# One issue order for the attention's cycle, or one for each of three stages

## The chip, the cores and the metric

The kernel runs on one core of a Trainium2 chip. The metric is the device time of one execution in microseconds (us); the number compared is the median over several runs of the same kernel.

## The reference, cut to what matters

Two branches work on the same 2048 x 640 input and are mixed by a gate per row. Branch A is attention with 32 heads of width 20, branch B is a Fourier mixing: a DFT along the features, then one along the sequence, of which the real part is kept.

```python
g = sigmoid((x * gate_w).sum(-1, keepdims=True))          # x = A_x, 2048 x 640
q, k, v = split(x @ wqkv)                                 # 32 heads of 20
o = softmax(q @ k.T * 20 ** -0.5) @ v                     # per head, 2048 x 2048 scores
a = concat_heads(o) @ wo
f_re, f_im = x @ dft_hid_re.T, x @ dft_hid_im.T           # feature DFT
b = dft_seq_re @ f_re - dft_seq_im @ f_im                 # sequence DFT, real part
return g * a + (1 - g) * b
```

(The input B_x is handed in but not read.)

## The kernel before, in words

The kernel writes its instruction streams by hand: no scheduler reorders anything, and each engine takes its instructions in the order in which the Python code issues them.

After some 270 us of projections (q, k, v and the first tiles of the feature DFT) a loop of 256 cycles follows (L849). It carries the attention and, in the gaps, the Fourier branch and the output projection. An attention "unit" is a pair of heads and half of the queries; there are 32 units of 8 cycles each, a cycle is 4 steps, and a step covers two heads.

One cycle issues four kinds of work to TensorE, in the order of a string of letters, `ORDER` (L36, read in L850 to L856):

- `e` (L830): a score matmul, keys x queries, 128 x 512, whose result ScalarE turns into exp (L832) and writes to the tile `p`. A cycle has 8.
- `m` (L168): a score matmul the other way round, queries x keys, 128 x 512, of which VectorE takes the row maxima (L170). These run `LEAD` = 41 steps ahead of the `e` for the same scores, since the maxima must be known first. A cycle has 8.
- `F` (`fill`, L774): some steps of the other branch. A step is a pair of matmuls of 320 columns, one on each half of the array, that add into the PSUM tiles `yp0` and `yp1`. In the feature DFT (`hid_tile`, L346) a cycle has 15 steps, in the sequence DFT (`dft_step`, L575) 16, and in the output tiles (`out_tile`, L646) 12. The steps of a cycle are spread over the `F` places of the string in equal shares (L759 to L764).
- `B` (`burst`, L836): the 16 matmuls that multiply `p` with `v` (L494), and whatever reads a finished `yp` out (L839; ScalarE reads one half and VectorE adds the other).

Array halves: a head has 20 rows, three copies are stacked to 60 rows (62 with the maxima), and so a score matmul uses 64 of the 128 rows of the array: rows 0 to 63 for one head of the pair ("half 0"), rows 64 to 127 for the other ("half 1"). The two heads of a step are issued one after the other. Which one comes first is set by the table `FIRST` (L37), one entry for each of the four steps of a cycle, read in L816. A fill step has one matmul for each half, half 0 first.

PSUM banks: all scores, `e` and `m` alike, take their banks from one ring of five (`bank`, L122). So score number k of a cycle can be loaded only after ScalarE or VectorE has read score k - 5.

The 256 cycles fall into three stages: 54 cycles beside the feature DFT (`HID` = 54), about 170 beside the sequence DFT (56 products of 3 cycles, and 2 more cycles at the first of them, whose first cycles have fewer steps: `RAMP`, L42), and 30 beside the output tiles. In the last ten cycles no `m` is left to issue.

Of the kernel before, what the change touches and what calls it, by code (L numbers as in the profile page):

```python
# [32 lines left out]

ORDER = "emFemFFFFemFeFFmeFFemFFFmmFFmeeB"  # L36
FIRST = {"e": (0, 0, 1, 1), "m": (1, 1, 1, 1)}  # L37


LEAD = 41  # L40
# [32 lines left out]
def mix_kernel(ctx: ExitStack, tc: tile.TileContext, xa, wqk, wb, cdft, wo, out):  # L73
# [48 lines left out]
    def bank():  # L122
        return ps_w.tile([P, 512], F32, name=f"ps{next(turn) % 5}")
# [23 lines left out]
    def q_unit(n):  # L147
        u = n % 2 * (S // 2)
        return qst[n // 2 % 2][:, u : u + S // 2]
# [8 lines left out]
    def s_mm(i, h):  # L158
        n, s = divmod(i, 32)
        if n >= NU:  # L160
            return lambda: None
        qt, kc = divmod(s, 4)
        q, k = q_unit(n), kst[(n // 2) % 2]
        if n not in mx:
            mx[n] = small.tile([P, 2, 8, 4], F32, name="mx", bufs=2)
        ps = bank()
        b = 64 * h
        pe.matmul(ps, q[b : b + KROWS, qt * P : (qt + 1) * P],  # L168
                  k[b : b + KROWS, kc * 512 : (kc + 1) * 512], start=True, stop=True)
        return lambda: dve.tensor_reduce(mx[n][:, h, qt, kc : kc + 1], ps, axis=AX.X, op=ALU.max)  # L170

    def s_end(i):
        n, s = divmod(i, 32)
        if n < NU and s == 31:
            if now[0] < 0:
                max_nm(n)
            else:
                ends.append(n)
        if s == 1 and 0 < n <= NU and now[0] < 0:
            max_chain(n - 1)  # L180
# [237 lines left out]
    for n, c in enumerate(order):  # L418
        for t in range(4):
            m = 4 * n + t  # L420
# [317 lines left out]
    HID = 4 * NS - HEAD  # L738
# [10 lines left out]
    edge = [first]  # L749
    for u in range(UNITS):  # L750
        k, t = LONG[u // HT], u % HT
        edge.append(edge[-1] + (2 if u == 0 else 0) + 3 + k * (t + 1) // HT - k * t // HT)
    cycles += [(edge[u], edge[u + 1], 3 * NS) for u in range(UNITS)]
    cycles += [(edge[-1] + u, edge[-1] + u + 1, 3 * (ND - 1)) for u in range(2 * len(PRE))]
    assert cycles[-1][1] <= last + 1
    at_goal = 0
    for c0, c1, count in cycles:
        for c in range(c0, c1):
            share = count * (c + 1 - c0) // (c1 - c0) - count * (c - c0) // (c1 - c0)  # L759
            if c0 == first:  # L760
                share = RAMP[c - c0]
            places = ORDER.count("F")
            goals[c] = [at_goal + share * (f + 1) // places for f in range(places)]
            at_goal += share  # L764

    for k, tt in enumerate(PRE):
        i = 4 * (edge[-1] + 2 * k)
# [6 lines left out]
    def fill(c):  # L774
        nonlocal done
        goal = goals[c].pop(0) if c in goals else 0
        while done < goal:
            next(fills)
            done += 1

    def begin(i):
        now[0] = i
        n, s = divmod(i, 32)
        for fn in later.pop(i, ()):
            fn()
        if s % 2 == 0:
            flush()
        if s == 0 and n % 2 == 0:
            p = n // 2
            if p + 1 < NP:  # L790
                at_step(i + 6, functools.partial(load_v, p + 1))
                for j, args in enumerate(load_stack(p + 1)):
                    at_step(i + 2 + j, functools.partial(sp.dma_start, *args))
        if i < total:
            pts[n, s // 2, s % 2] = pair_tile()

    def end(i):
        if start < i <= start + HT:
            for k in range(2):
                at_step(i + 3, load_a(0, 2 * (i - start - 1) + k))  # L800
        if i % 4 == 2:
            c = i // 4
            if c + HEAD in (NS, 2 * NS):
                at_step(i + 2, load_wb(3 + (c + HEAD) // NS, pool, pool))
            if c in (HID - 7, HID - 5, HID - 3):
                at_step(i + 4, load_c((c - HID + 7) // 2))
        if i in LAST:
            LAST[i]()
# [3 lines left out]
    def score(kind):  # L812
        x = heads[kind]
        heads[kind] += 1
        i, z = divmod(x, 2)
        h = z ^ FIRST[kind][(i - (LEAD if kind == "m" else 0) - 1) % 4]  # L816
        if kind == "m":
            s_mm(i, h)()
            if z:
                s_end(i)  # L820
            return
        if z == 0 and i <= total:
            begin(i)
        if i < total:
            n, s = divmod(i, 32)
            kt, qc = divmod(s, 2)
            q, k = q_unit(n), kst[(n // 2) % 2]
            b = 64 * h
            pt = bank()
            pe.matmul(pt, k[b : b + KROWS + 2, kt * P : (kt + 1) * P],  # L830
                      q[b : b + KROWS + 2, qc * 512 : (qc + 1) * 512], start=True, stop=True)
            act.activation(pts[n, kt, qc][:, h], pt, AF.Exp, scale=float(DH) ** -0.5)  # L832
            if z:
                end(i)

    def burst(c):  # L836
        for n in ends:
            max_nm(n)
        run_extras(max(done - HIDS, 0) // 3, 2)  # L839
        for kt in (2 * c, 2 * c + 1):  # L840
            av_step(now[0], kt // NS, kt % NS)
        while ends:
            max_chain(ends.pop(0))
        if c == HID - 1:
            start_dft()

    for kind in "emme":
        score(kind)
    for c in range(total // 4):  # L849
        for kind in ORDER:  # L850
            if kind == "F":
                fill(c)
            elif kind == "B":
                burst(c)
            else:
                score(kind)  # L856
# [124 lines left out]
```

## Time and profile before

| | |
|---|---|
| median of 3 runs | 1891.77 us |
| lowest, highest run | 1891.42, 1894.12 us |
| span of the profiled execution | 1888.5 us |
| TensorE matmul busy | 1877.4 us (99% of the span) |
| VectorE, ScalarE, GpSimd busy | 1470.0, 1219.1, 1005.1 us |
| DMA | 280.50 MB, mean 149 GB/s |

The times are device times of whole executions; the span runs from the first to the last instruction in one profiled execution, and that execution has no other time of its own in the page. What lies around the span is put at 1891.77 - 1888.5 = 3.3 us here.

In the profile's rows, PE is a matmul and PEld the load of its weights. The engine letters are PE (TensorE), DVE (VectorE), ACT (ScalarE), POOL (GpSimd), SP (the queue that issues most DMAs). A row of the timeline gives the start in us, the time from the first start to the last end of the merged instructions, engine, line, operation, tiles and how many. A matmul's time in a row is longer than its turn on the array, because consecutive matmuls overlap; the turn is read from the distance between starts.

### The profile page before, as it was taken

What the parts mean: (1) busy time and instruction counts of PE and PEld (TensorE: products, weight loads), DVE (VectorE), ACT (ScalarE), POOL (GpSimd) and SP (SyncE); (2) the same over time, 40 slices, a digit from 0 to 9 for tenths busy, and PEclk for the clock granted to TensorE, in tenths of its full rate; (3) what the DMA queues carried; (4) which work ended last, traced back from release to release, by engine and by line L of the source; (5) the groups of instructions that cost most, each with busy time, mean ns of one, the idle gap of its engine ahead of it and who ended that gap; (6) DMA issues with size and microseconds to landing.
All of it is one profiled execution on the core that took longest, in us unless ns stands there. A gap on an engine that the chain in (4) does not pass through costs nothing. (4 is left out here: it accounts for less than half of the span.)

```text
span 1888.5 us, 44537 instructions
## 1 busy us (share of the span) xinstructions
PE 1877.4 (99%) x17453; PEld 1358.2 (72%) x17453; DVE 1470.0 (78%) x2445; ACT 1219.1 (65%) x2350; POOL 1005.1 (53%) x872
## 2 busy tenths in 40 slices
PE   9999999999999999999999999999999999999998
PEld 8987777777776677776767677776767677766666
DVE  4145569989898888888888888888888888889954
ACT  4221147777777767666767667666767676677785
POOL 1200001010004999466699989958879988734343
PEclk9999999999999999999999999999999999999999
DMA  7843341221215575536557576736475746442214
GB/s 232 181 133 128 128 154 48 62 76 49 75 58 147 163 238 178 148 123 169 180 176 238 171 234 190 201 119 189 156 220 195 225 147 205 154 114 70 62 49 157
DMA packets 174804, 280.50 MB, mean 149 GB/s; under 512 B 44303, under 2 KB 106895, under 8 KB 174595
## 3 DMA queue, kind: packets, MB, share of 16 engines
q1 hardware_dynamic: 173635, 275.70, 47.7%
q0 software_dynamic: 960, 1.97, 0.6%
q8 instruction: 137, 2.24, 0.5%
q14 instruction: 72, 0.59, 0.1%
HBM read 213.37 MB, written 63.52 MB: 147 GB/s over the span
## 5 line engine op out<-in xcount | busy, mean ns | idle before, releaser
L170 DVE TENSOR_REDUCE mx<-ps 128x1 f32<-128x512 f32 x2048 | 1294.8, 684 | 175.8 <-PE ps L168 154.8
L832 ACT ACTIVATE p<-ps 128x512 f32<-128x512 f32 x2048 | 1087.0, 599 | 432.7 <-PE ps L168 223.6
L168 PE MATMUL ps<-kst,qst 60*128 60x512 f32 x2048 | 785.2, 415 | 3.7 <-DVE mx L170 1.7
L830 PE MATMUL ps<-qst,kst 62*128 62x512 f32 x2048 | 698.9, 413 | 0.5 <-ACT p L832 0.3
L575 PE MATMUL yp<-a,part 64*128 64x320 f32 x5376 | 649.1, 307 | 0.0
L575 PEld LDWEIGHTS yp<-a,part 64*128 64x128 f32 x5376 | 582.2, 186 | 7.3
L494 PE MATMUL av<-p,v 128*21 128x512 f32 x4096 | 491.3, 596 | 0.0
L830 PEld LDWEIGHTS ps<-qst,kst 62*128 62x128 f32 x2048 | 335.7, 185 | 200.9 <-DVE mx L170 182.4
L168 PEld LDWEIGHTS ps<-kst,qst 60*128 60x128 f32 x2048 | 371.2, 184 | 24.7 <-DVE mx L170 9.6
L113 POOL TENSOR_TENSOR part<-raw,part 128x1024 fp32r<-128x1024 f32 (+1 forms) x129 | 290.4, 2251 | 10.3
L494 PEld LDWEIGHTS av<-p,v 128*21 128x21 f32 x4096 | 98.4, 100 | 226.7 <-issue 223.2
L346 PE MATMUL yp<-wb,xs 64*128 64x320 f32 x1920 | 236.0, 308 | 0.1
L112 POOL CAST part<-raw 128x1024 fp32r<-128x1024 f32 (+1 forms) x129 | 127.0, 985 | 161.5 <-PE yp L575 141.2
L346 PEld LDWEIGHTS yp<-wb,xs 64*128 64x128 f32 x1920 | 206.0, 186 | 4.5 <-DVE raw L355 0.5
L465 POOL TENSOR_TENSOR raw<-raw,raw 128x1024 f32<-128x1024 f32 x77 | 185.4, 2408 | 6.4 <-DMA raw<-in_cdft 4.8
L112 POOL CAST wb<-raw 128x966 fp32r<-128x966 f32 (+1 forms) x4 | 3.4, 862 | 255.4 <-DMA raw<-in_wb 255.4
L524 POOL TENSOR_TENSOR o<-o,rb 128x512 f32<-128x512 f32 x31 | 40.2, 1296 | 146.6 <-DMA rb<-r_scr 100.8
L113 POOL TENSOR_TENSOR a<-araw,a 128x320 fp32r<-128x320 f32 x112 | 97.6, 872 | 9.0
L113 DVE TENSOR_TENSOR p<-ps,p 128x512 fp32r<-128x512 f32 x40 | 27.5, 691 | 93.5 <-ACT p L110 90.8
L646 PE MATMUL yp<-a,part 64*128 64x320 f32 x720 | 89.5, 309 | 0.0
L110 ACT ACTIVATE p<-ps 128x512 fp32r<-128x512 f32 x40 | 23.7, 597 | 100.6 <-PE ps L118 100.6
L646 PEld LDWEIGHTS yp<-a,part 64*128 64x128 f32 x720 | 76.9, 186 | 2.5
(86 smaller groups left out, 1237.0 us busy)
## 6 DMA issues: line engine op xcount, KB each, us to landing
raw<-in_cdft SPq DMA_DIRECT2D x192, 512.0 KB
araw<-a_scr SPq DMA_DIRECT2D x192, 160.0 KB
qk_scr<-p SPq DMA_DIRECT2D x40, 512.0 KB
kst<-qk_scr SPq DMA_DIRECT2D x90, 160.0 KB
qst<-qk_scr SPq DMA_DIRECT2D x90, 160.0 KB
a_scr<-raw SPq DMA_DIRECT2D x64, 160.0 KB
yt<-y_scr SPq DMA_DIRECT2D x64, 160.0 KB
y_scr<-yt SPq DMA_DIRECT2D x64, 160.0 KB
```

What stands on the lines that cost most here:

```text
L112: e1.tensor_copy(dst1, src)
L113: e2.tensor_tensor(dst2, src, f32(dst1), op=ALU.subtract)
L168: pe.matmul(ps, q[b : b + KROWS, qt * P : (qt + 1) * P], k[b : b + KROWS, kc * 512 : (kc + 1) * 512], start=True, stop=True)
L170: return lambda: dve.tensor_reduce(mx[n][:, h, qt, kc : kc + 1], ps, axis=AX.X, op=ALU.max)
L346: pe.matmul(yp[h][:, :HE], xs[r, xz, d, cs], w[r, wz, d, :HE], start=d == 0 and z == 0, stop=d == ND - 1 and z == 2)
L465: pool.tensor_tensor(raws[0], raws[0], raws[1], op=ALU.add if PRODUCTS[n][0][1][0] > 0 else ALU.subtract)
L494: pe.matmul(av[32 * j : 32 * j + DH + 1, :], v[:, kt, h * (DH + 1) : (h + 1) * (DH + 1)], pp[qc][:, h, :], start=kt == 0, stop=kt == NS - 1)
L524: pool.tensor_tensor(o, o, rb, op=ALU.mult)
L575: pe.matmul(yp[h][:, :HE], c[r, cz, cs], a[r, az], start=s == 0 and z == 0, stop=s == NS - 1 and z == 2)
L646: pe.matmul(yp[h][:, :HE], o[r, oz, d], wos[d, hf][r, wz], start=d == 0 and z == 0, stop=d == ND - 2 and z == 2)
L830: pe.matmul(pt, k[b : b + KROWS + 2, kt * P : (kt + 1) * P], q[b : b + KROWS + 2, qc * 512 : (qc + 1) * 512], start=True, stop=True)
L832: act.activation(pts[n, kt, qc][:, h], pt, AF.Exp, scale=float(DH) ** -0.5)
```

## The change

Instead of one order and one table for all 256 cycles there are three, chosen by the cycle's number: for the feature DFT (`hid`), the sequence DFT (`seq`) and the output tiles (`out`). Each has its own string and its own choice of which array half each step takes first. The number of `F` places differs (9, 7 and 13 instead of 15), so a place takes more than one step. The counts of every kind of instruction stay as they were.

```diff
-ORDER = "emFemFFFFemFeFFmeFFemFFFmmFFmeeB"
-FIRST = {"e": (0, 0, 1, 1), "m": (1, 1, 1, 1)}
+ORDERS = {
+    "hid": ("emFmeFFemFeFmeFemFFmeFmmeB", {"e": (0, 0, 1, 1), "m": (1, 1, 1, 0)}),
+    "seq": ("ememFFemFemFmeFemFFmeemB", {"e": (1, 1, 1, 1), "m": (0, 0, 0, 0)}),
+    "out": ("ememFFFFemeFFmeFFemFFFmmFFmeeB", {"e": (0, 0, 1, 1), "m": (1, 1, 1, 1)}),
+}
...
+    def play(c):
+        return ORDERS["hid" if c < HID else "seq" if c < edge[-1] else "out"]
+
...
-            places = ORDER.count("F")
+            places = play(c)[0].count("F")
...
-        h = z ^ FIRST[kind][(i - (LEAD if kind == "m" else 0) - 1) % 4]
+        c, k = divmod(i - (LEAD if kind == "m" else 0) - 1, 4)
+        h = z ^ play(c)[1][kind][k]
...
-        for kind in ORDER:
+        for kind in play(c)[0]:
```

Written out with the half behind each score, and with as many F as there are steps (one F is a pair of matmuls, one for each half), a full cycle of each stage is issued like this:

```
hid before  e0 m1 F e1 m0 FFFF e0 m1 F e1 FF m0 e1 FF e0 m1 FFF m0 m1 FF m0 e1 e0 B
hid after   e0 m1 F m0 e1 FFFF e0 m1 F e1 FF m0 e1 FF e0 m1 FFF m0 e1 FF m0 m1 e0 B
seq before  e0 m1 F e1 m0 FFFF e0 m1 F e1 FF m0 e1 FF e0 m1 FFF m0 m1 FFF m0 e1 e0 B
seq after   e1 m0 e0 m1 FFFF e1 m0 FF e0 m1 FFF m0 e1 FF e0 m1 FFFFF m0 e1 e0 m1 B
out before  e0 m1 e1 m0 FFFF e0 m1 e1 FF m0 e1 FF e0 m1 FF m0 m1 FF m0 e1 e0 B
out after   e0 m1 e1 m0 FFF e0 m1 e1 FF m0 e1 FF e0 m1 FFF m0 m1 FF m0 e1 e0 B
```

(With 12 steps on 15 or 13 places some places of the string stay empty in the output stage.)

## The prediction

> **What bounds the kernel now.** I read the page first, its busy shares and its two costliest groups.
>
> ```profile
> span 1888.5 us, 44537 instructions
> PE 1877.4 (99%) x17453; PEld 1358.2 (72%) x17453; DVE 1470.0 (78%) x2445; ACT 1219.1 (65%) x2350; POOL 1005.1 (53%) x872
> L170 DVE TENSOR_REDUCE mx<-ps 128x1 f32<-128x512 f32 x2048 | 1294.8, 684 | 175.8 <-PE ps L168 154.8
> L832 ACT ACTIVATE p<-ps 128x512 f32<-128x512 f32 x2048 | 1087.0, 599 | 432.7 <-PE ps L168 223.6
> L575 PE MATMUL yp<-a,part 64*128 64x320 f32 x5376 | 649.1, 307 | 0.0
> ```
>
> PE is covered by matmuls, and both readers of the scores wait for PE. But "busy" counts a matmul from its start to its last result, and a matmul on one half of the array hides idle time on the other. So 99% proves neither that the array is full nor that nothing else holds it up. For that I need single cycles.
>
> Next the busy time by stretch: the cycles beside the feature DFT, beside the sequence DFT, and the first of the output stage. Under it the same stretches for line L494 alone, whose matmuls come 16 to a cycle.
>
> ```profile
> 269.00:603.30 334.30, 334.19 (x3298) 237.56 (x3294) 299.93 (x505) 245.99 (x485) 34.41 (x22) 1.00 0.26 76
> 628.00:1686.30 1058.30, 1058.30 (x10691) 751.72 (x10689) 888.64 (x1476) 740.44 (x1412) 847.57 (x681) 1.00 0.58 178
> 1692.40:1790.00 97.60, 97.60 (x896) 65.36 (x896) 89.31 (x152) 74.71 (x146) 39.49 (x50) 1.00 0.28 80
> ```
>
> ```profile
> 269.00:603.30 334.30, 101.48 (x848) 20.21 (x848) 1.00 0.26 76
> 628.00:1686.30 1058.30, 319.76 (x2672) 63.63 (x2672) 1.00 0.58 178
> 1692.40:1790.00 97.60, 30.63 (x256) 6.09 (x256) 1.00 0.28 80
> ```
>
> The columns are the stretch, its length, then busy time and count of PE, PEld, DVE, ACT, POOL (in the second answer PE and PEld only), the granted clock, DMA share and GB/s. Cycles: 848 / 16 = 53 of 6.31 us, 2672 / 16 = 167 of 6.34 us, 256 / 16 = 16 of 6.10 us. In the long stretch DVE is busy 84%, POOL 80%, ACT 70%; the clock is full. What one cycle loses or gains there counts about 165 times, so that stage decides.
>
> Now one cycle of the sequence DFT, PE's rows of the timeline; the second fence holds three rows of the same cycle from the timeline of all engines.
>
> ```profile
> 902.16 0.49 PE L830 MATMUL ps<-qst,kst 62*128 62x512 f32 x1
> 902.16 0.49 PE L168 MATMUL ps<-kst,qst 60*128 60x512 f32 x1
> 902.50 0.31 PE L575 MATMUL yp<-a,part 64*128 64x320 f32 x2
> 902.64 0.39 PE L168 MATMUL ps<-kst,qst 60*128 60x512 f32 x1
> 902.64 0.39 PE L830 MATMUL ps<-qst,kst 62*128 62x512 f32 x1
> 902.88 0.75 PE L575 MATMUL yp<-a,part 64*128 64x320 f32 x8
> 903.47 0.39 PE L830 MATMUL ps<-qst,kst 62*128 62x512 f32 x1
> 903.47 0.43 PE L168 MATMUL ps<-kst,qst 60*128 60x512 f32 x1
> 903.70 0.46 PE L575 MATMUL yp<-a,part 64*128 64x320 f32 x3
> 903.88 0.39 PE L830 MATMUL ps<-qst,kst 62*128 62x512 f32 x1
> ...
> 906.29 0.42 PE L830 MATMUL ps<-qst,kst 62*128 62x512 f32 x2
> 906.64 1.92 PE L494 MATMUL av<-p,v 128*21 128x512 f32 x16
> ```
>
> ```profile
> 902.73 4.53 DVE L170 TENSOR_REDUCE mx<-ps 128x1 f32<-128x512 f32 x7 [1.16 <-PE ps L168]
> 902.75 3.24 ACT L832 ACTIVATE p<-ps 128x512 f32<-128x512 f32 x6 [1.24 <-PE ps L168]
> 903.40 0.18 PEld L168 LDWEIGHTS ps<-kst,qst 60*128 60x128 f32 x1
> ```
>
> The prices are in it. A fill takes (0.75 - 0.307) / 3 = 0.148 us of its half (8 fills are 4 on each half). A score takes 903.70 - 903.47 = 0.23. The first pair after the burst takes 902.50 - 902.16 = 0.34, since its weights load in the open: 0.11 more. So each half needs 8 x 0.23 + 16 x 0.148 = 4.21 us plus 0.11. It had 906.29 - 902.16 + 0.23 = 4.36, or 4.39 for the later of the last two (their row is 0.42 long, a single one 0.39). **Only 0.04 to 0.07 us of a cycle is lost between the burst's end and the next burst**; the rest is work, or lies at the edges of the burst, where both strings have scores on either side.
>
> The one place where the scores nearly wait: score 5 (counting from 0; the `m` at 903.47) needs the bank of score 0. Its exp starts at 902.75 and lasts 0.599, so until 903.35; the weights load at 903.40; the matmul starts at 903.47, together with its neighbour. The bank came just in time.
>
> **The change, part by part.**
>
> *Sequence DFT, 165 full cycles.* The new order opens with four scores and four fill steps, and then wants score 5: one fill step earlier than before. The output stage already opens so (`e0 m1 e1 m0 FFFF e0 m1`), and its rows, from the timeline of all engines, show the cost:
>
> ```profile
> 1737.42 0.50 PE L830 MATMUL ps<-qst,kst 62*128 62x512 f32 x1
> 1737.42 0.73 PE L168 MATMUL ps<-kst,qst 60*128 60x512 f32 x2
> 1737.99 0.75 PE L646 MATMUL yp<-a,part 64*128 64x320 f32 x8
> 1738.01 3.12 ACT L832 ACTIVATE p<-ps 128x512 f32<-128x512 f32 x6 [0.90 <-PE ps L168]
> 1738.58 0.39 PE L830 MATMUL ps<-qst,kst 62*128 62x512 f32 x1
> 1738.67 0.18 PEld L168 LDWEIGHTS ps<-kst,qst 60*128 60x128 f32 x1
> 1738.67 0.50 PE L168 MATMUL ps<-kst,qst 60*128 60x512 f32 x1
> 1739.01 0.39 PE L830 MATMUL ps<-qst,kst 62*128 62x512 f32 x1
> 1739.15 0.18 PEld L168 LDWEIGHTS ps<-kst,qst 60*128 60x128 f32 x1
> ```
>
> Time from the first score: score 4 starts at 1738.58 - 1737.42 = 1.16, as 0.34 + 0.23 + 4 x 0.148 gives. Score 5 could start then too, but the first exp ends at 1738.01 + 0.60 = 1738.61 and its weights load at 1.25. Matmul and load start together, it is 0.50 long instead of 0.39, and the next score of that half comes 1739.01 - 1738.67 = 0.34 later instead of 0.23. The half loses 0.09 + 0.11 = 0.20. In the new sequence order score 5 is `m0`: half 0 loses 0.20. Behind the blocked load stand all later matmuls of PE's program, but half 1 has score 4 to work on until 1.39.
>
> Score 7 (`m1`) needs the bank of score 2, the second exp. Half 1 reaches it at 1.16 + 0.23 + 2 x 0.148 = 1.69. In the rows above score 7 also waits for the second exp and loads at 1739.15 - 1737.42 = 1.73, in the open: 0.04 + 0.11 = 0.15 lost on half 1. (Before, score 7 came at 904.14 or later, 1.98 from the start, by its row further down in the same answer:)
>
> ```profile
> 904.14 0.39 PE L168 MATMUL ps<-kst,qst 60*128 60x512 f32 x1
> ```
>
> After that nothing is late by these prices but perhaps the last `m1`. It needs the sixth exp, that of score 10. Half 0 starts score 10 at 1.36 + 3 x 0.23 + 7 x 0.148 = 3.09; an exp starts some 0.48 after its score (902.75 - 902.16 less the 0.11), so it ends near 4.17, and the load may go at 4.22; half 1 wants to start that matmul at 4.24. That is as tight as 903.40 to 903.47 above, and I count nothing for it here.
>
> Sum: half 0 needs 4.21 + 0.11 + 0.20 = 4.52, half 1 4.47. The burst waits for the later one: 4.52 against 4.36 to 4.39 is 0.13 to 0.16 us per cycle; I take 0.14, and 165 x 0.14 = 23.1 us.
>
> What the new order does better is that every fill step finds both halves level. Before, half 1 had a score ahead in most of the cycle. That can be worth at most the loss of 0.04 to 0.07 found above, and 4.52 already contains it as won.
>
> The readout of `yp` comes on every third cycle only and, since four scores now precede the first fill, has 0.23 more time than before: nothing. The tail ends in `m1` instead of `e1 e0`: DVE's last maximum starts later, but its bank is used again only by the fifth score after the burst (at 1.16), more than 2 us away, as the burst alone lasts 1.92: nothing. ACT's last exp comes earlier: nothing, it isn't on the path. The `e` steps that carry the DMA issues on SP stay in the same cycle and move by some tenths of a us; SP's queue and POOL (80% busy, with its loads issued cycles ahead) aren't near a bound, and a slower cycle gives both more room.
>
> *Feature DFT, 54 cycles.* Written out with its steps, the order differs in two swaps: scores 2 and 3, and scores 12 and 14 (`m1 .. e1` become `e1 .. m1`). Each is a swap of equal matmuls. Score 7 now needs the second maximum's bank instead of the second exp's. If that wait just bites, it costs up to the 0.11 of an open load, 54 x 0.11 = 6 us; on the other side, a cycle of 15 steps should take 6.34 - 0.148 = 6.19 and takes 6.31, so at most 0.12 x 54 = 6.5 us could be won, if the earlier last exp lets the readout end sooner. The row nearest to it is score 5's just-in-time load, at a cost near nothing: I take 0.
>
> *Output tiles, 30 cycles.* One step moves from before score 4 to after score 9. Score 5 still waits for the first exp to 1.25, so the moved step's time turns into waiting, and later scores have 0.148 more air. Between -0.148 and +0.148 on 20 cycles, 3 us either way: I take 0. The last ten cycles have no `m`: nothing.
>
> Total: 1888.5 + 23.1 = 1911.6 for the profiled execution, and with the 3.3 us between its span and the median, **1914.9 us**.
>
> **The rivals.**
>
> *The halves decide (faster).* If the banks come free in time, 0.04 is won in 165 cycles: 1891.8 - 6.6 = 1885.2. It decides if the first two exps free their banks 0.2 us earlier than in the rows above. For it: the new order is visibly the more even. Against it: the first exp cannot start before the first score has ended, in any order, and both stages show the same 1.24 to 1.25. The Trainium skill ("TensorE: Matmul & The Clock Gate", Part 3) says that matmuls start and end strictly in program order. By that rule an uneven order would idle a half, and evening it out would be the gain. The trace disagrees: the program has one step, two fills, between the `m` at 903.47 and the `e` at 903.88, but three fills start in between, so one half ran past the other. And the rule could not give more than the measured loss, 1885 again. Chance 0.12 for both.
>
> *Waits without the open load.* If the delayed scores load behind other work, score 5 costs 0.09 and score 7 0.04: half 0 needs 4.41, that is 0.02 to 0.05 or so more, with some unevenness 0.06: 165 x 0.06 = 10, 1902. Against it: the 0.50 and the 0.34 above. Chance 0.17.
>
> *A third wait.* If the last `m1` loads in the open or other scores miss their bank too, up to 0.11 more: 165 x 0.25 = 41, 1933. Chance 0.11.
>
> *No effect:* gains elsewhere cancel it, or the order isn't what I read: 1892. The written-out programs do differ as shown. Chance 0.04.
>
> **How the numbers follow.** Forecast 1914.9 with 0.56. Range 1898 to 1927: it takes in 0.04 to 0.21 us per cycle, so most of the second rival and half of the third. Runs of this kernel agree within 0.14%, so I call under 0.2% (3.8 us) the same. Faster 0.12, same 0.04, slower 0.84.
>
> **What would show it.** In the sequence stage the first `m` behind the four steps starts with its load, about 1.25 after the cycle's first score and 0.50 long; another at about 1.73; from first score to burst 0.13 to 0.16 more than 906.64 - 902.16 = 4.48; 6.47 to 6.50 us per cycle; the other stages at 6.31 and 6.10. I am wrong if cycles of the sequence stage are no longer than 6.34, or if score 5 loads before 1.1.

## The result, and the profile after

The changed kernel takes 1918.06 us (median of 4 runs, 1914.93 to 1921.49), the kernel before 1892.94 us in the same comparison. The ratio is 1.0132, 95% interval 1.0118 to 1.0147: 25.1 us slower, where 23.1 were forecast.

The page of the changed kernel, the lines that answer to those shown of before:

```profile
span 1912.8 us, 44634 instructions
PE 1901.4 (99%) x17453; PEld 1366.3 (71%) x17453; DVE 1450.9 (76%) x2445; ACT 1248.5 (65%) x2350; POOL 1005.3 (53%) x872
L175 DVE TENSOR_REDUCE mx<-ps 128x1 f32<-128x512 f32 x2048 | 1280.8, 683 | 228.9 <-PE ps L173 216.1
L842 ACT ACTIVATE p<-ps 128x512 f32<-128x512 f32 x2048 | 1116.8, 599 | 422.7 <-PE ps L173 347.0
```

The shares hardly move. PE is "99% busy" in a kernel that spends 24 us more; the shares alone don't show where. (The lines have moved: L840 is the score `e`, before L830; L173 is `m`, before L168; L580 the sequence fills, before L575; L842 the exp; L499 the product with v.)

The busy time by stretch, all engines, and below it line L499 alone; the stretches are those of before, moved by what came ahead of them.

```profile
269.00:602.30 333.30, 333.30 (x3297) 234.44 (x3295) 294.80 (x506) 248.37 (x485) 34.41 (x23) 1.00 0.26 76
627.50:1710.60 1083.10, 1083.10 (x10690) 763.05 (x10689) 875.29 (x1476) 767.65 (x1412) 846.44 (x679) 1.00 0.57 174
1716.60:1814.00 97.40, 97.40 (x893) 65.25 (x893) 89.15 (x152) 74.12 (x146) 39.38 (x50) 1.00 0.28 80
```

```profile
269.00:602.30 333.30, 101.47 (x848) 20.18 (x848) 1.00 0.26 76
627.50:1710.60 1083.10, 319.75 (x2672) 63.59 (x2672) 1.00 0.57 174
1716.60:1814.00 97.40, 30.63 (x256) 6.09 (x256) 1.00 0.28 80
```

The same 53, 167 and 16 cycles as before. Feature DFT 333.3 us instead of 334.3, output stage 97.4 instead of 97.6, sequence DFT 1083.1 instead of 1058.3. That stage is 24.8 us longer, and the whole span 24.3; a cycle takes 6.49 us instead of 6.34.

One cycle of that stage, PE's timeline, and then the loads and exps of the same cycle from the timeline of all engines:

```profile
895.12 0.49 PE L840 MATMUL ps<-qst,kst 62*128 62x512 f32 x1
895.13 0.72 PE L173 MATMUL ps<-kst,qst 60*128 60x512 f32 x2
895.47 0.40 PE L840 MATMUL ps<-qst,kst 62*128 62x512 f32 x1
895.69 0.76 PE L580 MATMUL yp<-a,part 64*128 64x320 f32 x8
896.28 0.39 PE L840 MATMUL ps<-qst,kst 62*128 62x512 f32 x1
896.36 0.50 PE L173 MATMUL ps<-kst,qst 60*128 60x512 f32 x1
896.51 0.65 PE L580 MATMUL yp<-a,part 64*128 64x320 f32 x4
896.85 0.49 PE L173 MATMUL ps<-kst,qst 60*128 60x512 f32 x1
897.00 0.39 PE L840 MATMUL ps<-qst,kst 62*128 62x512 f32 x1
...
899.17 0.61 PE L173 MATMUL ps<-kst,qst 60*128 60x512 f32 x2
899.40 0.40 PE L840 MATMUL ps<-qst,kst 62*128 62x512 f32 x1
899.73 0.63 PE L499 MATMUL av<-p,v 128*21 128x512 f32 x4
```

```profile
895.71 1.65 ACT L842 ACTIVATE p<-ps 128x512 f32<-128x512 f32 x3 [1.05 <-PE ps L173]
896.36 0.18 PEld L173 LDWEIGHTS ps<-kst,qst 60*128 60x128 f32 x1
896.85 0.18 PEld L173 LDWEIGHTS ps<-kst,qst 60*128 60x128 f32 x1
```

Score 4 starts 896.28 - 895.12 = 1.16 us after the first score. Score 5 loads at 1.24, just behind the end of the first exp (895.71 + 0.60 = 896.31), in the open, and its matmul lasts 0.50 instead of 0.39. Score 7 does the same at 1.73. From the first score to the burst: 899.73 - 895.12 = 4.61, before 4.48.

In all 167 cycles the mean from the first score to the burst is 4.615 us (before 4.466), from the burst's start to the next first score 1.871 in both. Scores of 0.47 us or longer, a mark of a load in the open, are 2.1 a cycle before (the pair after the burst) and 4.0 after.

### The profile page after: what moved, and what is told of

Its sections match the earlier page's. It is cut to its first block, busy times and chain, and to the rows that moved or that the text cites. A ratio compares the mean times of both kernels' runs of the same rounds, so it can differ in the third digit from the quotient of the medians.

```text
span 1912.8 us, 44634 instructions
## 1 busy us (share of the span) xinstructions
PE 1901.4 (99%) x17453; PEld 1366.3 (71%) x17453; DVE 1450.9 (76%) x2445; ACT 1248.5 (65%) x2350; POOL 1005.3 (53%) x872
## 5 line engine op out<-in xcount | busy, mean ns | idle before, releaser
L175 DVE TENSOR_REDUCE mx<-ps 128x1 f32<-128x512 f32 x2048 | 1280.8, 683 | 228.9 <-PE ps L173 216.1
L842 ACT ACTIVATE p<-ps 128x512 f32<-128x512 f32 x2048 | 1116.8, 599 | 422.7 <-PE ps L173 347.0
L173 PE MATMUL ps<-kst,qst 60*128 60x512 f32 x2048 | 798.1, 432 | 3.9 <-DVE mx L175 1.7
L840 PE MATMUL ps<-qst,kst 62*128 62x512 f32 x2048 | 752.3, 410 | 0.8 <-ACT p L842 0.3
L580 PE MATMUL yp<-a,part 64*128 64x320 f32 x5376 | 585.5, 306 | 0.0
L580 PEld LDWEIGHTS yp<-a,part 64*128 64x128 f32 x5376 | 525.8, 186 | 21.0
L840 PEld LDWEIGHTS ps<-qst,kst 62*128 62x128 f32 x2048 | 352.2, 185 | 198.3 <-DVE mx L175 145.6
L499 PE MATMUL av<-p,v 128*21 128x512 f32 x4096 | 491.3, 596 | 0.0
L173 PEld LDWEIGHTS ps<-kst,qst 60*128 60x128 f32 x2048 | 357.5, 184 | 32.1 <-DVE mx L175 9.1
L499 PEld LDWEIGHTS av<-p,v 128*21 128x21 f32 x4096 | 98.3, 100 | 224.2 <-issue 220.7
L351 PEld LDWEIGHTS yp<-wb,xs 64*128 64x128 f32 x1920 | 202.1, 186 | 4.5 <-DVE raw L360 0.2
L651 PE MATMUL yp<-a,part 64*128 64x320 f32 x720 | 89.9, 310 | 0.0
L651 PEld LDWEIGHTS yp<-a,part 64*128 64x128 f32 x720 | 77.8, 186 | 2.6
```

The costliest lines, as they stand in the source:

```text
L173: pe.matmul(ps, q[b : b + KROWS, qt * P : (qt + 1) * P], k[b : b + KROWS, kc * 512 : (kc + 1) * 512], start=True, stop=True)
L351: pe.matmul(yp[h][:, :HE], xs[r, xz, d, cs], w[r, wz, d, :HE], start=d == 0 and z == 0, stop=d == ND - 1 and z == 2)
L499: pe.matmul(av[32 * j : 32 * j + DH + 1, :], v[:, kt, h * (DH + 1) : (h + 1) * (DH + 1)], pp[qc][:, h, :], start=kt == 0, stop=kt == NS - 1)
L580: pe.matmul(yp[h][:, :HE], c[r, cz, cs], a[r, az], start=s == 0 and z == 0, stop=s == NS - 1 and z == 2)
L651: pe.matmul(yp[h][:, :HE], o[r, oz, d], wos[d, hf][r, wz], start=d == 0 and z == 0, stop=d == ND - 2 and z == 2)
L840: pe.matmul(pt, k[b : b + KROWS + 2, kt * P : (kt + 1) * P], q[b : b + KROWS + 2, qc * 512 : (qc + 1) * 512], start=True, stop=True)
```

## The experiments

The theory under test: a score that wants its bank before the bank's reader is done loses that wait plus an open load, and nothing else in the new order costs. The rivals: the choice of array halves, the other two stages, the grouping of the fills, the string's ends. "Halves" and "string" below are the table and the letters of the sequence stage. A cycle's mean from first score to burst, over 167 sequence cycles of each trace, is called its head; the scores of 0.47 us or longer in a cycle are its open loads.

| run | ratio to before, 95% interval | head, us | open loads |
|---|---|---|---|
| before | 1 | 4.466 | 2.1 |
| after | 1.0132 [1.0118, 1.0147] | 4.615 | 4.0 |
| x2_halves_only | 0.9996 [0.9986, 1.0005] | 4.466 | 2.1 |
| x3_string_only | 1.0287 [1.0270, 1.0305] | 4.789 | 5.0 |
| x4_opening | 1.0122 [1.0107, 1.0137] | 4.594 | 3.1 |
| x5_opening_short6 | 1.0017 [1.0007, 1.0026] | 4.476 | 2.1 |
| x6_short12 | 1.0005 [0.9995, 1.0015] | 4.463 | 2.1 |
| x7_short1236 | 0.9979 [0.9970, 0.9988] | 4.440 | 2.1 |
| x9_step_moved | 1.0129 [1.0114, 1.0144] | 4.609 | 3.0 |
| x11_seq_spaced | 0.9982 [0.9973, 0.9991] | 4.442 | 2.1 |

**Which stage (x1_seq_old).** The changed kernel with the old order in the sequence stage:

```diff
-    "seq": ("ememFFemFemFmeFemFFmeemB", {"e": (1, 1, 1, 1), "m": (0, 0, 0, 0)}),
+    "seq": ("emFemFFFFemFeFFmeFFemFFFmmFFmeeB", {"e": (0, 0, 1, 1), "m": (1, 1, 1, 1)}),
```

> The new orders in the feature DFT and output stages, the old order and halves in the sequence stage. Theory (two bank waits in the sequence stage carry all of it): the 25 us are gone; the traces of before and after put the feature stage at -1.1 us and the output stage at 0, so 0.999 of before, about 1892. Rival (part of the loss is carried over from the other stages or sits at the stage borders): 1897 or more.

1892.39 us, ratio 1.0000 [0.9990, 1.0009]. All of the loss is in the sequence stage; the other two new orders cannot be told from the old ones.

**Halves or string (x2_halves_only, x3_string_only).** Before, with half of the new sequence order each:

```diff
-    "seq": (old string, {"e": (0, 0, 1, 1), "m": (1, 1, 1, 1)}),
+    "seq": (old string, {"e": (1, 1, 1, 1), "m": (0, 0, 0, 0)}),                        # x2
+    "seq": ("ememFFemFemFmeFemFFmeemB", {"e": (0, 0, 1, 1), "m": (1, 1, 1, 1)}),      # x3
```

> Before, but in the sequence stage the new table of array halves (e always half 1 first, m always half 0 first) with the old string. Theory (the waits come from when a bank is wanted, so from the string): sequence cycles stay near 6.31, total within 4 us of before, 1889 to 1897. Rival (the choice of halves makes the loss): most of the 25 us, 1905 or more. Rival (even halves are a gain that the string spoils): up to 0.04 us in 165 cycles, 1886.

> Before, but in the sequence stage the new string with the old table of halves. Theory: score 5 still waits for the first exp at 1.25 us from the first score and score 7 for the second at 1.73, so at least the 25 us: 1917, and if the uneven halves (two scores of one half behind each other after the third group of fills) cost as well, up to 1930. Rival (the halves make the loss): near 1893.

x2: 1891.38 us, no difference. x3: 1946.45 us, twice the loss, and outside of what I expected. So the string makes the loss, and the new halves do no harm but save about half of what this string would cost with the old ones. (With the old string the new table is nearly a mirror image: written out, x2 is the cycle of before with half 0 and half 1 exchanged, but for the last four `e`.) The trace of x3 says why it is slower still (PE, one cycle, first score at 904.49; below it a row of ACT):

```profile
907.28 0.41 PE L840 MATMUL ps<-qst,kst 62*128 62x512 f32 x2
...
908.78 0.40 PE L840 MATMUL ps<-qst,kst 62*128 62x512 f32 x1
908.85 0.50 PE L173 MATMUL ps<-kst,qst 60*128 60x512 f32 x1
909.27 0.63 PE L499 MATMUL av<-p,v 128*21 128x512 f32 x4
```

```profile
907.71 1.09 ACT L842 ACTIVATE p<-ps 128x512 f32<-128x512 f32 x2 [0.31 <-PE ps L840]
```

Two `e` start together at 2.79, one on each half, so that their exps, the fifth and the sixth, queue. The sixth ends at 907.71 + 1.09 = 908.80, 4.31 from the start, and the last score, which needs its bank, loads in the open at 4.36, the fifth open load of the cycle. With the new halves the sixth exp ends at 4.11 (median of the cycles of after).

**Taking the first two waits away by the order (x4_opening).** Before, with the new halves and the new string behind the old opening:

```diff
+    "seq": ("emFemFFFFemFFemFFFmeFFemFFFFmeemB", {"e": (1, 1, 1, 1), "m": (0, 0, 0, 0)}),
```

> Before, but in the sequence stage the new halves and the new string with the old opening: em F em FFFF em, then FF em FFF me FF em FFFF me em. Scores 4 and 5 are wanted at 1.31 us, scores 6 and 7 at 1.84, when their banks (1.25, 1.73) are free. Theory (the two waits are the whole loss): cycles back at 6.31 or a little below, total 1886 to 1894. Rival (pairs of e and m level on both halves make one score after another wait for its reader; the next would be score 9, which needs the third exp): half or more of the loss stays, 1905 to 1917, and the trace shows the first two waits gone and open loads (matmuls of 0.5 us) at later scores.

1914.73 us, ratio 1.0122: the rival, in its time. But the wait that counts is not at score 9. From the timelines of PE and of all engines, rows of one cycle:

```profile
899.70 0.50 PE L840 MATMUL ps<-qst,kst 62*128 62x512 f32 x1
...
901.02 0.40 PE L840 MATMUL ps<-qst,kst 62*128 62x512 f32 x1
901.02 0.42 PE L173 MATMUL ps<-kst,qst 60*128 60x512 f32 x1
901.26 0.48 PE L580 MATMUL yp<-a,part 64*128 64x320 f32 x4
901.55 0.39 PE L173 MATMUL ps<-kst,qst 60*128 60x512 f32 x1
...
902.22 0.44 PE L840 MATMUL ps<-qst,kst 62*128 62x512 f32 x1
...
903.61 0.63 PE L840 MATMUL ps<-qst,kst 62*128 62x512 f32 x2
903.87 0.50 PE L173 MATMUL ps<-kst,qst 60*128 60x512 f32 x1
```

```profile
903.22 0.60 ACT L842 ACTIVATE p<-ps 128x512 f32<-128x512 f32 x1
903.87 0.18 PEld L173 LDWEIGHTS ps<-kst,qst 60*128 60x128 f32 x1
904.29 0.14 PEld L499 LDWEIGHTS av<-p,v 128*21 128x21 f32 x8 [0.24 <-issue]
```

Scores 4, 5 and 7 start on time. Score 9 (902.22) lasts 0.44 instead of 0.39 and so loses little. The last score would go behind the score ahead of it on its half, at 903.61 + 0.23 = 903.84; it needs the bank that the sixth exp reads until 903.22 + 0.60 = 903.82, loads in the open at 903.87 and holds the burst up until 904.29. In all, x4's head is 0.128 us longer than that of before, nearly as much as with the two open loads of the changed kernel (0.148).

**Freeing single banks (x5_opening_short6, x6_short12, x7_short1236).** Some exps of each sequence cycle take half of their columns, so that their bank is free about 0.2 us earlier: in x5 the sixth, in the kernel of x4_opening; in x6 the first two and in x7 the first, second, third and sixth, both in the changed kernel. The product with `v` reads the 256 columns that are there twice, so the matmuls that PE issues stay as many and as long; the result leaves out the other half of these scores. The lines of the exp (those of the product with `v` are not shown):

```diff
-            act.activation(pts[n, kt, qc][:, h], pt, AF.Exp, scale=float(DH) ** -0.5)
+            cut = HID <= (i - 1) // 4 < edge[-1] and 2 * ((i - 1) % 4) + z in (5,)     # (0, 1); (0, 1, 2, 5)
+            w = 256 if cut else 512
+            act.activation(pts[n, kt, qc][:, h, :w], pt[:, :w], AF.Exp, scale=float(DH) ** -0.5)
```

> The kernel of x4_opening, but the sixth exp of every cycle in the sequence stage takes 256 of its 512 columns (the p times v matmul then reads these 256 twice); its bank comes free some 0.25 us earlier. In x4_opening the first two waits were gone and only the last score of a cycle still loaded in the open, 4.17 us from the first, when score 10's bank (read by the sixth exp) came free. Theory (that third wait alone is what is left of the loss): cycles at 6.31, total 1888 to 1896. Rival (the level pairs cost in their middle): 1905 to 1915.

> The changed kernel, but the first two exps of every cycle in the sequence stage take 256 of 512 columns, so that scores 5 and 7 find their banks free. Theory (three waits stand behind each other, each worth about the same): the last score now waits for the sixth exp as in x4_opening, and 1908 to 1917 stays. Rival (the prediction's: these two waits are all): 1886 to 1895.

> The changed kernel, but the first, second, third and sixth exps of every cycle in the sequence stage take 256 of 512 columns. Theory (the loss is nothing but scores that wait for the reader of their bank): all waits are gone and the string is as good as the old one, 1884 to 1895. Rival (something else in the new string costs, such as the order at the edges of the burst): 1900 or more.

x5: 1895.73 us, ratio 1.0017. The third wait was most of what was left in x4; about 3 us over before stay. x6: 1892.86 us, ratio 1.0005. Here my revised theory failed and the recorded prediction held: freeing the first two banks brings everything back, and the third wait doesn't bind. The rows of x6 (first score at 891.45; L845 is the score `e` here, L851 the exp) show why:

```profile
892.05 0.66 ACT L851 ACTIVATE p<-ps 128x256 f32<-128x256 f32 x2 [1.09 <-PE ps L173]
892.62 0.40 PE L845 MATMUL ps<-qst,kst 62*128 62x512 f32 x1
892.63 0.39 PE L173 MATMUL ps<-kst,qst 60*128 60x512 f32 x1
...
893.12 2.27 ACT L851 ACTIVATE p<-ps 128x512 f32<-128x512 f32 x4 [0.41 <-PE ps L845]
...
895.43 0.18 PEld L173 LDWEIGHTS ps<-kst,qst 60*128 60x128 f32 x1
...
895.61 0.39 PE L173 MATMUL ps<-kst,qst 60*128 60x512 f32 x1
```

The short exps release score 5 with score 4, at 1.18. Scores 4 to 11 run 0.14 to 0.18 earlier than in x4_opening (medians of the cycles), and the last four at about the same time, since one more fill step stands ahead of them. The third to the sixth exp run back to back (one row, of four), so that the sixth is done at 893.12 + 2.27 = 895.39, 3.94 from the start instead of 4.12 in x4_opening, and the last score's load at 895.43 is hidden. x7: 1888.00 us, ratio 0.9979 [0.9970, 0.9988]: with these four exps short the new string takes 0.027 us a cycle less than the old one. What x5 and x6 keep over x7, 0.036 and 0.024 us a cycle, fits score 9, which waits for the third exp: it lasts 0.43 us in both (median), and 0.39 in x7, where that exp is short.

**The opening by itself (x9_step_moved).** Before, with one fill step moved from ahead of score 2 to behind score 5, old halves:

```diff
-    "seq": ("emFemFFFFemFeFFmeFFemFFFmmFFmeeB", ...
+    "seq": ("ememFFFFemFFeFFmeFFemFFFmmFFFmeeB", ...
```

> Before, but in the sequence stage one fill step is moved from between the first two pairs of scores to behind score 5: em em FFFF em FF e FF m e FF em FFF mm FFF m e e, old halves. Theory (a score 5 that is wanted before 1.25 us costs its half 0.20, and the later half sets the cycle): +0.13 to 0.16 us per cycle, 1912 to 1918. Rival (one wait on one half is made up by the free running of the halves): up to 1900.

1916.42 us, ratio 1.0129 [1.0114, 1.0144]. One fill step, moved from ahead of score 2 to behind score 5, makes as large a loss as the whole change: score 5 loads 1.24 from the start (one cycle, timeline of all engines):

```profile
897.91 0.50 PE L840 MATMUL ps<-qst,kst 62*128 62x512 f32 x1
...
899.15 0.18 PEld L173 LDWEIGHTS ps<-kst,qst 60*128 60x128 f32 x1
899.16 0.50 PE L173 MATMUL ps<-kst,qst 60*128 60x512 f32 x1
```

**Orders without waits (x10_hid_out, x11_seq_spaced, x12_all_spaced, x13_hid_seq).** Orders laid out so that, by the prices, fewer scores are wanted before their bank is free. x10 has new ones in the feature and the output stage, x11 in the sequence stage, x12 in all three, x13 in the feature and the sequence stage:

```diff
+    "hid": ("ememFFFeFFmeFFFmeFFmeFFFmmFFmeeB", {"e": (1, 1, 0, 0), "m": (0, 0, 1, 1)}),
+    "seq": ("ememFFFFeFFmFemFFeFFmeFFmFmFFeemB", {"e": (0, 0, 0, 0), "m": (1, 1, 1, 1)}),
+    "out": ("emFemFFFeFmeFFmeFmFemFmFmFeeB", {"e": (1, 1, 1, 0), "m": (0, 0, 1, 1)}),
```

> Before, with other orders in the feature DFT (em em FFF e FF me FFF me FF me FFF mm FF m e e) and in the output stage, laid out so that by the prices of the rows (0.23 a score, 0.148 a fill, 0.11 an open load, 1.25 and 1.73 us for the first two exps' banks) fewer scores wait; the sequence stage as before. Theory (a score's wait for its bank is the one loss that an order can take away): the feature cycles shrink from 6.25 towards 6.18 and the output cycles by up to 0.02, 54 x 0.07 + 20 x 0.02 = 4 us, 1886 to 1891. Rival (the feature cycles' 0.06 lie elsewhere): 1892.

> Before, with a sequence order that opens like the changed kernel (four scores, four fill steps) but puts a single e next and score 5 two steps later (em em FFFF e FF m F em FF e FF me FF m F m FF e e m). Theory (the opening costs nothing by itself; what costs is the wait): no open loads after the burst's first pair, 0.02 to 0.04 us won in 165 cycles, 1885 to 1890. Rival (an opening of four scores costs by itself): 1900 or more.

> The orders of x10_hid_out and x11_seq_spaced together. Theory: the two gains add up, 1881 to 1887, a version faster than both kernels. Rival: no gain, 1892.

> The feature order of x10_hid_out and the sequence order of x11_seq_spaced, the output stage with its old order. In x12_all_spaced the feature cycles took 6.21 us (before 6.29 in the runs of that chip) and the sequence cycles 6.31, but the output cycles 6.25 instead of 6.13, with open loads at scores 10 and 12. Theory: the new output order gave back some 2 us, which return: 1884 to 1888. Rival (the gain of x12 is all that there is): 1887.7 as x12.

x10: 1890.89 us, 0.9993 [0.9984, 1.0002], not told from before. Its trace shows two effects that go against each other: feature cycles of 6.22 us instead of 6.31, but output cycles of 6.23 instead of 6.13 (means of 53 feature cycles and of the 20 output cycles with `m`, from first score to first score). x11: 1889.02 us, 0.9982 [0.9973, 0.9991], a gain, with four scores in a row and four fill steps at the opening like the changed kernel. So the opening costs nothing when no wait follows it. x12: 1887.70 us, 0.9977 [0.9967, 0.9986], a little less than expected; the slower output cycles (6.23) are in it. x13: 1886.75 us, **0.9959 [0.9945, 0.9972]**: 0.4% faster than before by its own comparison; that it also beats x12 is not shown, as the intervals overlap.

## Why the prediction was right

*The stage and the term.* 23.1 us were forecast in the sequence stage and nothing elsewhere; the traces show 24.8 there, -1.0 and -0.2 in the others, and x1 confirms it. The cycle's loss is 0.148 (4.6146 - 4.4663), inside the 0.13 to 0.16 worked out. The price read from the output stage's rows held to a hundredth: load at 1.24 and 1.73 (1.25 and 1.73 forecast), matmuls of 0.50 and 0.49. With these two rows the rival of waits without the open load fell. The 3.3 us put around the span were too many: the profiled execution of the changed kernel took 1914.93 us with a span of 1912.8, 2.1 apart.

*That the two waits carry it*: right (x6). x9 shows that one would have been enough, as "the burst waits for the later half" implies: two open loads on different halves cost hardly more than one (0.148 against 0.143).

*The third wait, counted at nothing because it looked tight*: right for this order, but partly by luck. The sum has the load at 4.22 and the matmul wanted at 4.24, 0.02 apart; an open load costs 0.11, so by these prices half 1 would have come to 4.47 + 0.09 = 4.56, 0.04 more than the 4.52 of half 0. What made the wait harmless is that an exp starts 0.43 after a score whose load is hidden (median for score 10 of after), not 0.48. The rows of the sixth exp and the last score's load, in the cycle of after shown above:

```profile
898.13 1.09 ACT L842 ACTIVATE p<-ps 128x512 f32<-128x512 f32 x2
899.28 0.18 PEld L173 LDWEIGHTS ps<-kst,qst 60*128 60x128 f32 x1
```

The exp ends at 899.22, 4.10 from the start, and the load goes at 4.16. Its matmul starts at 4.27 (median), 0.10 behind the load, and lasts 0.40, so hardly any of the load is in the open. x4 shows the same wait at the price of an open load, with the load at 4.17, where the matmul is wanted at 4.14. I then took the three waits for independent and expected x6 to stay slow; it did not, since earlier exps move the sixth exp too.

*Level halves, at most 0.04 a cycle*: x7 measures 0.027 with four exps short, so the bound held. That the gain comes from level halves is not shown: x11 wins 0.024 with whole exps, in an order in which one half is a score ahead at four groups of fills, just as in before. In before, score 5 lasts 0.43 us (median), and both x7 and x11 have it at 0.40. x2 is no test of it, as its order is as uneven as that of before. What I had not seen is that with this string the old halves would have been worse by 0.17 a cycle (x3 against after).

*The rival of the halves, with the rule of strict program order* fell with the sign of the result: the banks did not come 0.2 us earlier. The rows of after speak against the rule as well. Score 6 (`e0`) stands ahead of score 7 (`m1`) in the program, but starts at 897.00, behind it (896.85), and so it is in 165 of the 167 cycles. x2 can't decide it, since its order is nearly the mirror image of the old one.

*Feature and output stages at zero*: right within the noise of x1. The 0.12 that I had left as the most the feature cycles could win was partly there, but not in the order of this change, whose feature cycles took 6.29 us against 6.31 before: with the other order of x10, x12 and x13 they took 6.22, 6.22 and 6.24.

## What to carry to other kernels

With a short ring of buffers, write down for each place in the order when the producer wants its buffer and when the reader gives it back; one fill step of 0.148 us, moved past such a point, cost 1.3% here (x9), while no busy share moved by more than a point. Price a wait from another stage of the same kernel that already has it, load in the open included. Where one wait is removed, work the later ones out again: they may take its place at the full price (x4), or go away with it (x6).

## What the runs showed that I had not expected

How much of a load is hidden sets the price, more than the length of the wait. In the sequence cycles of before, after, x4, x5, x6 and x9 a score lasts 0.39 to 0.40 us when its weights start to load 0.10 us or more ahead of its matmul, 0.43 at 0.07, 0.45 at 0.05 and 0.50 at 0 (medians): what the neighbours don't hide of some 0.11 us of load is added to it. So a wait of 0.08 us costs a cycle 0.148, and one of 0.03 us or less at the end still most of 0.128 (x4). And one open load on one half costs a cycle nearly as much (x9: 0.143 over before) as two on different halves (0.148).
